# Induced attention and a squared-ReLU feed-forward: elementwise steps over four f-tiles, one transpose per unit, list-scheduled order

## The chip, the cores and the metric

The kernel runs on one core of a Trainium2 chip. The metric is the device time of one execution in microseconds (us), here the median of three runs. The engines of the core are TensorE (PE; PEld is its weight load), VectorE (DVE), ScalarE (ACT), GpSimd (POOL) and SyncE (SP, which issues the DMAs). Each works through its own instructions in the order in which the program issues them, and they wait for each other on semaphores.

## What is computed

From `x` (4 x 12480 x 128), 32 inducing points and the two matrices of a feed-forward layer (128 x 2048 and 2048 x 128):

```python
def mab(q, kv):
    s = scale * (q @ kv.transpose(0, 2, 1))
    s = s - s.max(-1, keepdims=True)
    a = np.exp(s)
    a /= a.sum(-1, keepdims=True) + 1e-09
    return a @ kv
h = mab(I, x)          # first attention: inducing points over all tokens
y = mab(x, h)          # second attention: tokens over the inducing points
...
h = np.maximum(y @ w_in, 0.0)
return (h * h @ w_out)
```

`x` and the inducing points are float32; the weights reach the kernel as float64 words and are turned into float32 on the chip. Nearly all arithmetic is in the two products of the feed-forward layer.

## The kernel before

A batch of 12480 tokens is cut into 13 **units** of 960 tokens, a unit into two **blocks** of 480, the hidden width 2048 into 16 **f-tiles** of 128. There are 52 units. The main loop runs over batches and units; in unit u of batch b the engines also do the first attention of unit u of batch b+1 and the second attention's weights of the next unit. Batch 0's first attention and the conversion of the weights stand ahead of the loop.

- **Feed-forward** (`ffn_block`). The tile `hw` is h @ w_in, split in a rounded part and its rest; `st` holds the second attention's weights, split likewise, with the parts stacked on the 128 partitions as (hi, lo, hi, lo). For each pair of f-tiles two *wide* products (L508, 480 columns) fill a PSUM tile `h`. ACT takes `r` = relu(h) (L515) and `g` = r squared (L522), both 128 x 960; DVE or POOL rounds `g` to `hi` (L593 or L595); DVE forms `lo` = g - hi (L530). Six *narrow* products (L543) add up hi x wo_hi, hi x wo_lo and lo x wo_hi in the PSUM tile `op`. One pair of each unit (marked "f" in `HI`) is not split: its two narrow products take `g` and `wo_f` in plain float32. Of a unit's other 15 pairs POOL rounds 5, DVE 10. At a block's end `op` is copied (`ot`), transposed (`otp`, L569) and scaled into `osb` (L577), which SP stores.
- **Second attention** (`second_unit`): four products `s` (L420, 32 columns of the array each), copied, transposed (`s2t`), the softmax's maximum, difference and exponential (`d`), then POOL writes the rounded weights *twice* and DVE and POOL their rest, so that `sk` holds the stack (hi, lo, hi, lo). Four transposes for each block (`ap`, L477; eight in a unit) turn it, and one copy per block gives `st`.
- **First attention** (`first_unit`): eight transposes `xtp`, four products `sp` (L278), maximum, exponential, two transposes `ep`, eight products `hp` (L324, 32 columns each), and an update of the running sum. `s`, `sp` and `hp` use 32 of the array's columns; everything else uses them all.
- **Order.** Each step is put at a position on a clock of pairs of f-tiles by tables of numbers (`S_MAIN`, `T_MAIN`, `AT_G2` and others); the program sorts the steps by that position and issues them so. Buffers: two PSUM tiles for `h` (a pair each), two for `op`, two banks for all else; in SBUF 3 of `r`, 4 of `g`, 4 of `hi`, 3 of `lo`, each a pair.

Of the kernel before, what the change touches and what calls it, by code (L numbers as in the profile page):

```python
# [24 lines left out]
BLK = UNIT // 2   # tokens of a block, the width of the feed-forward products  # L25


@with_exitstack
def induced_attention_then_squared_relu_ffn(
# [17 lines left out]
    # engines, by pair of f-tiles in the first and the second block of a unit; "f": not split  # L47
    SQ = ('aaaaaaaa', 'aaaaaaaa')   # of the square
    HI = ('vpvpvvpf', 'vvpvvpvv')   # of the rounding
    # engines that empty PSUM  # L50
    XT, XT_EARLY, ET, SS, ST, OT = 'av', 'aa', 'a', 'v', 'av', 'vv'
    RB, GB, HB, LB = 3, 4, 4, 3
    AT_G1, AT_SQA, AT_SQV, AT_HIP, AT_HIA, AT_HIV, AT_LO, AT_G2, AT_G2D = -1.4, 1.05, 0.8, 1.1, 0.7, 1.2, 2.05, 3.3, 0.16
    AT_HI = {"p": AT_HIP, "a": AT_HIA, "v": AT_HIV}
    T_START = (-0.2, 0.3, 0.6, 0.7, 1.5, 1.7, 2.0, 2.4, 3.2, 3.3, 4.1, 4.5)
    T_MAIN = (1.1, 2.2, 2.9, 4.2, 7.2, 7.7, 8.02, 10.3, 10.5, 11.1, 13.4, 13.5)
    E_START = (-0.3, 0.0, 0.6, 0.8, 0.9, 1.0, 1.8, 2.9, 4.4, 4.8, 5.1, 6.1, 6.7, 7.6, 8.0)
    E_MAIN = (0.1, 0.6, 0.7, 1.4, 1.7, 2.1, 2.6, 5.2, 6.8, 8.5, 9.2, 9.3, 10.4, 11.1, 12.9)
    S_MAIN = (0.1, 1.8, 3.0, 3.2, 3.92, 5.2, 5.3, 6.02, 7.1, 7.2, 7.62, 8.1, 9.52, 9.6, 10.1, 10.3, 11.9)
    S_LAST = (0.4, 0.6, 2.7, 3.1, 4.62, 5.2, 5.8, 6.62, 6.9, 7.6, 7.62, 8.1, 8.62, 9.7, 10.0, 14.0, 14.5)  # L60
    S_START = (1.9, 2.1, 2.6, 3.2, 4.36, 4.75, 5.2, 5.26, 5.95, 6.0, 6.31, 6.75, 6.91, 7.35, 7.45, 8.85, 9.95)
    START, T_END, T_FFN, T_NEXT = 1.2, 3.5, 9, 8.5
    W_START = ((1.7, 0.306), (3.3, 0.42), (5.9, 0.504), (8.0, 0.588), (10.6, 0.5), (13.5, 0.35), (15.5, 0.847), (19.8, 0.425))
    O_MAIN = (0.0, 2.2, 2.5)
    AT_S2, AT_S1 = 0.05, 0.05
# [9 lines left out]
    ps_m = ctx.enter_context(tc.tile_pool(name="ps_m", bufs=2, space=PSUM))  # L75

# [3 lines left out]
    # token p * (N / TS) + j of a batch lies on partition p of sub-tile j  # L80
# [14 lines left out]
    # same_m[(q m), (k m')] = (m == m')  # L95
# [8 lines left out]
    # lane_q[(q m), q'] = (q == q')  # L104
# [13 lines left out]
    plan = []  # L118

    def at(t, fn):  # L120
        plan.append((t, len(plan), fn))
# [4 lines left out]
    # w_out's tiles for the products that are not split  # L126
    FULL = [p for p in range(NP) if "f" in (HI[0][p], HI[1][p])]
    wo_f = const.tile([P, 2 * max(len(FULL), 1), C], F32, name="wo_f")
# [6 lines left out]
    def weights(name, load, use, t0, step):  # L135
# [6 lines left out]
        shape = [P, WCH]  # L142

# [36 lines left out]
        def low():  # L180
            v["b"] = tile_of("b", F32)
            nc.vector.scalar_tensor_tensor(
                v["b"], v["w"][:, :, 0].bitcast(U32), 2.0 ** -52, v["power"].bitcast(F32),
                ALU.mult, ALU.mult,
            )
            use(v["a"].bitcast(F32), v["b"])

        at(t0 - 1.5, words)
        for i, fn in enumerate((clamp, size, flush, field, sign, power, low)):
            at(t0 + step * i, fn)  # L190
# [11 lines left out]
    def load_weights():  # L202
        n = F // WCH
        at(-10, open_stage)
        for k in range(n):
            sl = slice(k * WCH, (k + 1) * WCH)

            def load(t, sl=sl):
                nc.sync.dma_start(t, w_in[:, sl].bitcast(I32).rearrange("p (n two) -> p n two", two=2))

            def use(a, b, sl=sl):
                nc.gpsimd.tensor_add(w_in_sb[:, sl], a, b)

            weights(f"i{k}", load, use, *W_START[k])
        for k in range(n):
            m = WCH // C

# [6 lines left out]
            def use(a, b, k=k):  # L224
                hi = wo_hi[:, k * m:(k + 1) * m, :].rearrange("p f c -> p (f c)")
                lo = wo_lo[:, k * m:(k + 1) * m, :].rearrange("p f c -> p (f c)")
                for i, p in enumerate(FULL):
                    if m * k <= 2 * p < m * (k + 1):
                        sl = slice((2 * p - m * k) * C, (2 * p - m * k + 2) * C)
                        nc.gpsimd.tensor_add(  # L230
                            wo_f[:, 2 * i:2 * i + 2, :].rearrange("p f c -> p (f c)"),
                            a[:, sl], b[:, sl],
                        )
                nc.scalar.copy(hi, a)
                nc.gpsimd.tensor_sub(a, a, hi)
# [8 lines left out]
    # lane (q m): inducing point m over the sub-tiles 2q and 2q + 1 of each unit  # L244
    def first_unit(b, u, t0, ahead, times, early=False):
        v = {}
        n = f"{b}_{u}"
        s = state.setdefault(b, {"xt": []})

        def load():  # L250
            v["xn"] = load_x(b, u, pools["early"] if early else xn_pool)

        def turn(k):
            if k == 0:
                v["xt"] = xt_pool.tile([C, UNIT], F32, tag="xt", name=f"xt_{n}")
                s["xt"].append(v["xt"])
            if not early:
                v["tp"] = bank(f"xtp_{n}_{k}")
            else:
                v["tp"] = ps_o.tile([P, 512], F32, tag="o", name=f"xtp_{n}_{k}")  # L260
            tp = v["tp"]
            for t in range(4):
                nc.tensor.transpose(  # L263
                    tp[:, t * TS:(t + 1) * TS], v["xn"][:, 4 * k + t, :], ident[:TS, :TS]
                )

        def turned(k):
            part = v["xt"][:, k * BLK:(k + 1) * BLK]
            copy((XT_EARLY if early else XT)[k], part, v["tp"][:, :BLK])

        def score():
            if early:
                v["sp"] = ps_h.tile([P, 2, 512], F32, tag="h", name=f"sp_{n}")[:, 0, :]
            else:
                v["sp"] = bank(f"sp_{n}")
            sp = v["sp"]
            for q in range(Q):
                nc.tensor.matmul(  # L278
                    sp[q * M:(q + 1) * M, :2 * TS], indT,
                    v["xt"][:, q * 2 * TS:(q + 1) * 2 * TS], start=True, stop=True,  # L280
                )

        def top():
            v["mx"] = tiny.tile([P, 1], F32, tag="mx", name=f"mx_{n}")
            nc.vector.tensor_reduce(v["mx"], v["sp"][:, :2 * TS], axis=AX.X, op=ALU.max)  # L285

        def shift():
            # the maximum so far, times -scale
            v["neg"] = tiny.tile([P, 1], F32, tag="neg", name=f"neg_{n}", bufs=4)
            if u:  # L290
                v["before"] = s["neg"]
                nc.vector.scalar_tensor_tensor(
                    v["neg"], v["mx"], -scale, s["neg"], ALU.mult, ALU.min
                )
            else:
                nc.vector.tensor_scalar_mul(v["neg"], v["mx"], -scale)
            s["neg"] = v["neg"]

        def power():
            v["z"] = tiny.tile([P, 1], F32, tag="z", name=f"z_{n}")  # L300
            v["e"] = att.tile([P, 2 * TS], F32, tag="e1", name=f"e1_{n}")
            nc.scalar.activation(
                v["e"], v["sp"][:, :2 * TS], AF.Exp, bias=v["neg"], scale=scale, accum_out=v["z"]
            )
            if u:
                v["fade"] = tiny.tile([P, 1], F32, tag="fade", name=f"fade_{n}")
# [346 lines left out]
```

## Time and profile before

| | before |
|---|---|
| median of three runs | 1799.92 us (1798.96 to 1800.03) |
| span of the profiled execution | 1796.8 us |
| PE, DVE, ACT, POOL busy | 98%, 90%, 91%, 25% |

The profiled execution's own time isn't given apart from its span, first instruction to last; the median lies 3.1 us above the span. Busy time on PE overstates the work, since successive matmuls overlap; so the rows on PE below are pieces of the chain that ended last, in which every stretch of time is counted once. ACT's and DVE's instructions overlap a little too (one starts some 0.1 us before the end of the one ahead of it).

### The profile page before, as it was taken

What the parts mean: (1) busy time and instruction counts of PE and PEld (TensorE: products, weight loads), DVE (VectorE), ACT (ScalarE), POOL (GpSimd) and SP (SyncE); (2) the same over time, 40 slices, a digit from 0 to 9 for tenths busy, and PEclk for the clock granted to TensorE, in tenths of its full rate; (3) what the DMA queues carried; (4) which work ended last, traced back from release to release, by engine and by line L of the source; (5) the groups of instructions that cost most, each with busy time, mean ns of one, the idle gap of its engine ahead of it and who ended that gap; (6) DMA issues with size and microseconds to landing.
All of it is one profiled execution on the core that took longest, in us unless ns stands there. A gap on an engine that the chain in (4) does not pass through costs nothing.

```text
span 1796.8 us, 27067 instructions
## 1 busy us (share of the span) xinstructions
PE 1766.7 (98%) x9729; PEld 1422.9 (79%) x9729; DVE 1620.0 (90%) x2315; ACT 1628.0 (91%) x2070; POOL 442.8 (25%) x439
## 2 busy tenths in 40 slices
PE   7799999999999999999999999999999999999998
PEld 4478888888778888888878888888887888888887
DVE  6899989999989989989989989989989999999998
ACT  5699999999899999999988999999999999999997
POOL 1312222222222222222221222222222323233231
PEclk9899999999999999999999999999999999999999
DMA  8200100100100110100100110110100000000000
GB/s 214 57 23 23 44 23 23 45 23 23 45 23 23 37 31 23 45 23 23 45 23 23 28 39 23 35 33 23 38 19 12 23 12 23 12 16 19 12 23 23
DMA packets 16912, 57.07 MB, mean 32 GB/s; under 512 B 1704, under 2 KB 3784, under 8 KB 16776
## 3 DMA queue, kind: packets, MB, share of 16 engines
q1 hardware_dynamic: 16776, 55.34, 11.5%
q8 instruction: 76, 1.25, 0.3%
q14 instruction: 60, 0.49, 0.1%
HBM read 29.77 MB, written 25.56 MB: 31 GB/s over the span
## 4 chain that ended last, share of the span: by engine, by line
PE 95%; DVE 2%; DMA 1%; issue 0%; ACT 0%; SPq 0%; POOL 0%; ACTq 0%; DVEq 0%
PE op L543 62%; PE h L508 20%; PE otp L569 3%; PE ap L477 2%; PE xtp L263 2%; PE s L420 2%; PE hp L324 1%; PE sp L278 1%; PE wp L393 1%; DMA words_i<-in_moe_w_in_dram 1%; PE s2t L432 1%; DMA words_o<-in_moe_w_out_dram 1%; PE ep L312 1%; DVE lo L530 0%; DVE mx L285 0%
## 5 line engine op out<-in xcount | busy, mean ns | idle before, releaser
L530 DVE TENSOR_TENSOR lo<-g,hi 128x960 fp32r<-128x960 f32 x780 | 941.9, 1214 | 68.6 <-POOL hi L595 39.1
L515 ACT ACTIVATE r<-h 128x960 f32<-128x960 f32 x832 | 812.0, 976 | 96.8 <-PE h L508 93.7
L522 ACT ACTIVATE g<-r 128x960 f32<-128x960 f32 x832 | 839.6, 1009 | 0.0
L595 POOL TENSOR_SCALAR hi<-g 128x960 fp32r<-128x960 f32 x260 | 282.8, 1088 | 1112.0 <-ACT g L522 1058.1
L543 PE MATMUL op<-hi,wo_hi 128*128 128x480 f32 x1560 | 520.1, 407 | 0.0
L508 PE MATMUL h<-st,hw 128*128 128x480 f32 x1664 | 507.7, 386 | 0.0
L543 PE MATMUL op<-lo,wo_hi 128*128 128x480 f32 x1560 | 479.4, 383 | 0.0
L543 PE MATMUL op<-hi,wo_lo 128*128 128x480 f32 x1560 | 476.2, 381 | 0.0
L593 DVE CAST hi<-g 128x960 fp32r<-128x960 f32 x520 | 374.1, 719 | 3.4 <-ACT g L522 3.4
L543 PEld LDWEIGHTS op<-hi,wo_hi 128*128 128x128 f32 x1560 | 284.4, 189 | 91.7 <-issue 58.7
L508 PEld LDWEIGHTS h<-st,hw 128*128 128x128 f32 x1664 | 306.1, 189 | 47.7 <-issue 3.9
L543 PEld LDWEIGHTS op<-hi,wo_lo 128*128 128x128 f32 x1560 | 293.7, 188 | 43.6
L543 PEld LDWEIGHTS op<-lo,wo_hi 128*128 128x128 f32 x1560 | 293.5, 188 | 41.4 <-DVE lo L530 0.2
L595 POOL TENSOR_SCALAR sk<-d 120x256 fp32r<-120x256 f32 x104 | 102.5, 1001 | 86.3 <-ACT d L446 86.3
L593 DVE COPY ot<-op 128x480 f32<-128x480 f32 x104 | 67.9, 653 | 59.8 <-PE op L543 59.7
L543 PE MATMUL op<-g,wo_f 128*128 128x480 f32 x208 | 100.7, 565 | 0.0
L477 PEld LDWEIGHTS ap<-identr,sk 120*128 120x128 f32 x416 | 62.9, 192 | 26.2 <-issue 20.0
L477 PE MATMUL ap<-identr,sk 120*128 120x120 f32 x416 | 76.3, 306 | 2.0 <-POOL sk L595 2.0
L577 DVE TENSOR_TENSOR osb<-otp,zz 120x512 f32<-120x512 f32 x104 | 70.7, 680 | 2.9 <-PE otp L569 2.2
L263 PE MATMUL xtp<-ident,xn 120*128 120x120 f32 x416 | 63.9, 279 | 8.2 <-DMA xn<-in_x_dram 4.0
L263 PEld LDWEIGHTS xtp<-ident,xn 120*128 120x128 f32 x416 | 51.2, 147 | 22.3 <-ACT xt L591 5.1
L569 PE MATMUL otp<-ident,ot 128*120 128x128 f32 x416 | 63.8, 276 | 0.8 <-DVE ot L593 0.8
(89 smaller groups left out, 867.3 us busy)
## 6 DMA issues: line engine op xcount, KB each, us to landing
xn<-in_x_dram SPq DMA_DIRECT2D x52, 480.0 KB, 5.7
out_dram<-osb SPq DMA_DIRECT2D x52, 480.0 KB, 3.7
words_i<-in_moe_w_in_dram SPq DMA_DIRECT2D x4, 512.0 KB, 6.7
words_o<-in_moe_w_out_dram SPq DMA_DIRECT2D x4, 512.0 KB, 5.0
ind_sb<-in_inducing_dram SPq DMA_DIRECT2D x1, 16.0 KB, 1.7
```

What stands on the lines that cost most here:

```text
L263: nc.tensor.transpose(tp[:, t * TS:(t + 1) * TS], v["xn"][:, 4 * k + t, :], ident[:TS, :TS])
L420: nc.tensor.matmul(sp[q * M:(q + 1) * M, :2 * TS], s["hT"][:, :M], xt[:, q * 2 * TS:(q + 1) * 2 * TS], start=True, stop=True,)
L477: nc.tensor.matmul(ap[:, q * TS:(q + 1) * TS], v["sk"][:, k * Q + q].rearrange("t a k m -> t (a k m)"), identr[:TS, :TS], start=(q == 0), ...
L508: nc.tensor.matmul(v["hp"][:, i, :BLK], s["hw"][:, f * P:(f + 1) * P], s["st", u, k], start=True, stop=True,)
L515: nc.scalar.activation(v["r"], v["hp"][:, :, :BLK], AF.Relu)
L522: nc.scalar.activation(v["g"], v["r"], AF.Square)
L530: nc.vector.tensor_sub(v["lo"], v["g"], v["hi"])
L543: nc.tensor.matmul(w["op"][:, :BLK], wo[:, f, :], v[part][:, i, :], start=(p == 0 and j == 0), stop=(p == NP - 1 and j == len(steps) - 1),)
L569: nc.tensor.transpose(tp[:TS, q * P:(q + 1) * P], w["ot"][:, q * TS:(q + 1) * TS], ident)
L577: nc.vector.tensor_mul(s["osb", u].rearrange("t (q k) c -> t k q c", k=2)[:, k], w["tp"][:TS, :].rearrange("t (q c) -> t q c", q=Q), s["zz ...
L593: nc.vector.tensor_copy(dst, src)
L595: nc.gpsimd.tensor_scalar(dst, src, 1.0, 0.0, ALU.mult, ALU.add)
```

## The change

The parts, as the diff has them:

1. **Four f-tiles.** The relu still takes a pair (128 x 960) but writes into one half of a tile `g` of four f-tiles; the square is taken in place over 128 x 1920; `hi` and `lo` are formed over 128 x 1920, all on DVE. Buffers: 3 of `g`, 2 of `hi`, 2 of `lo`, each four f-tiles; `r` is gone. No pair is left unsplit: `wo_f` and its products are gone, and each unit has 96 narrow products of the split kind (90 before, and 2 in float32).
2. **One transpose.** `sk` is written once, as (block, hi/lo, m), by one rounding on ACT or DVE and one subtraction on DVE; four transposes in a unit instead of eight give both blocks' weights on 64 partitions each; one copy makes `sw`; four DMAs from SBUF to SBUF, issued by SP, write `st` with the stack doubled. POOL has no part in the main loop but the `sums` of each batch's end.
3. **Grouped narrow products.** `s` and `sp` of a unit go into one bank (`na`) and, with the eight `hp` of the first attention's unit before (`nb`), stand in a row on PE.
4. **Order.** A class `Plan` takes the steps with an engine (or a choice of ACT and DVE), a duration, a due time and what they need, and a greedy list scheduler fixes the order and the choice. Copies of `op` go to ACT in 99 of 104 cases (before, all to DVE); of `xt` 66 of 104 (before 65); of `sw` 17 of 52 (of `st` before, 52 of 104); the rounding of `sk` 46 of 52.

```diff
+    def run(self):
...
+                    key = (0.0 if start <= free[e] + 40.0 else start, t.due, t.order)
...
-    RB, GB, HB, LB = 3, 4, 4, 3
+    GB, HB, LB = 3, 2, 2
+    PERIOD, START, T_MAIN, NARROW, STEP = 32000.0, 2600.0, 66000.0, 6000.0, 1700.0
...
         def high():
-            v["sk"] = att.tile([TS, G, 2, 2, M], F32R, tag="sk", name=f"sk_{n}")
-            for k in range(2):
-                copy("p", v["sk"][:, :, k, 0, :], v["d"])
+                v["sk"] = att.tile([TS, Q, 2, 2, M], F32R, tag="sk", name=f"sk_{n}")
+                copy(th, v["sk"][:, :, :, 0, :], v["d"].rearrange("t (k q) m -> t q k m", q=Q))
...
-        def back(k):
-            v["ap"] = ap = bank(f"ap_{n}_{k}")
+            def back():
+                v["ap"] = ap = bank(f"ap_{n}")
                 for q in range(Q):
...
+            def spread():
+                st = att.tile([P, 2, BLK], F32R, tag="st", name=f"st_{n}")
+                for k in range(2):
+                    for j in range(2):
+                        nc.sync.dma_start(
+                            st[j * 64:(j + 1) * 64, k, :].bitcast(F32),
+                            v["sw"][k * 64:(k + 1) * 64, :].bitcast(F32),
+                        )
+                s["st", u] = st
...
+    def narrow(second, f, g, due, step, begun=None):
...
+            if second:
+                second.score(v["a"][:, :2 * TS])
+            if f:
+                f.score(v["a"][:, 2 * TS:4 * TS])
+            if g:
+                v["b"] = bank(f"nb_{g.n}")
+                g.mix(v["b"][:, :C])
...
             def relu():
-                v["r"] = pools["ffn"].tile([P, 2, BLK], F32, tag="r", name=f"r_{n}_{p}", bufs=RB)
-                nc.scalar.activation(v["r"], v["hp"][:, :, :BLK], AF.Relu)
+                    nc.scalar.activation(v["g"][:, 2 * i:2 * i + 2, :], c["hp"][:, :, :BLK], AF.Relu)
...
             def square():
-                    nc.scalar.activation(v["g"], v["r"], AF.Square)
+                nc.scalar.activation(v["g"], v["g"], AF.Square)
...
+            th = add("DVE", 1070, high, due + 5700, [sq], port=True, takes=[bhi], reads=[bg])
+            tl = add("DVE", 2076, low, due + 7800, [th], port=True, takes=[blo], reads=[bg, bhi])
...
+    for t in plan.run():
+        t.fn()
```

On PE in mid batch before, `s` of the next unit between narrow products of the block (names are tile_unit_block..., the batch left out):

```order
L508 MATMUL h_7_0_1_8396<-st_7_0_8269,hw_5477 128x480 x2
L543 MATMUL op_6_1_8303<-hi_6_1_4_8338,wo_lo 128x480 x2
L543 MATMUL op_6_1_8303<-lo_6_1_4_8370,wo_hi 128x480 x2
L420 MATMUL s_1_8_8409<-xt_8_3575,hT_5475 32x240 x4
L543 MATMUL op_6_1_8303<-hi_6_1_5_8375,wo_hi 128x480 x2
L508 MATMUL h_7_0_2_8418<-st_7_0_8269,hw_5477 128x480 x2
L543 MATMUL op_6_1_8303<-hi_6_1_5_8375,wo_lo 128x480 x2
```

And on PE in the changed kernel, where the three narrow groups of a unit stand:

```order
L755 MATMUL h_3_0_0_5915<-st_3_5793,hw_4764 128x480
L795 MATMUL op_2_1_5874<-hi_2_1_1_5892,wo_lo 128x480 x2
L599 MATMUL na_4_5923<-xt_4_1755,hT_4762 32x240 x4
L403 MATMUL na_4_5923<-xt_4_5818,indT 32x240 x4
L457 MATMUL nb_3_5932<-xn_3_5066,et_3_5724 32x128 x8
L795 MATMUL op_2_1_5874<-hi_2_1_1_5892,wo_lo 128x480 x2
L755 MATMUL h_3_0_1_5952<-st_3_5793,hw_4764 128x480
```

The groups that stood in three places of a unit, with full-width products on both sides, now stand in one; and a wide product stands between each two pairs of narrow ones.

On ACT in mid batch before, relu (L515) and square (L522) in turn:

```order
L515 ACTIVATE r_3_0_1_6940<-h_3_0_1_6912 128x960
L522 ACTIVATE g_3_0_0_6944<-r_3_0_0_6918 128x960
L515 ACTIVATE r_3_0_2_6965<-h_3_0_2_6934 128x960
L522 ACTIVATE g_3_0_1_6969<-r_3_0_1_6940 128x960
L591 COPY xt_4_6947<-xtp_4_0_6948 128x480
L515 ACTIVATE r_3_0_3_6988<-h_3_0_3_6957 128x960
L522 ACTIVATE g_3_0_2_6992<-r_3_0_2_6965 128x960
```

And on ACT in the changed kernel at the same stage, relu L763, square L774:

```order
L763 ACTIVATE g_3_0_1_5981<-h_3_0_2_5962 128x960
L763 ACTIVATE g_3_0_1_5981<-h_3_0_3_5974 128x960
L763 ACTIVATE g_3_0_2_5997<-h_3_0_4_5987 128x960
L429 ACTIVATE e_2_4_6011,z_4_6010<-na_4_5923,neg_4_5995 128x240
L432 ACTIVATE fade_4_6013<-neg_3_5685,neg_4_5995 128x1
L774 ACTIVATE g_3_0_1_5981<-g_3_0_1_5981 128x1920
L224 COPY et_4_6034<-ep_4_6023 120x256
L630 ACTIVATE d_4_6038<-d_4_6038 120x256
L224 CAST sk_4_6047<-d_4_6038 120x8x32
L224 COPY ot_2_1_6054<-op_2_1_5874 128x480
```

A square now covers two relus, and the copy `ot` and the rounding `sk` have moved here from DVE and POOL.

On SP in mid batch before, a load of `x` and a store of a unit's result in turn:

```order
L583 DMA out_dram<-osb_4_7622 120x1024
L86 DMA xn_7_7809<-in_x_dram 120x1024
L583 DMA out_dram<-osb_5_7993 120x1024
L86 DMA xn_8_8180<-in_x_dram 120x1024
L583 DMA out_dram<-osb_6_8364 120x1024
```

And on SP in the changed kernel:

```order
L830 DMA out_dram<-osb_2_5903 120x1024
L675 DMA st_4_6103<-sw_4_6087 64x480 x4
L369 DMA xn_7_6260<-in_x_dram 120x1024
L830 DMA out_dram<-osb_3_6213 120x1024
L675 DMA st_5_6413<-sw_5_6397 64x480 x4
L369 DMA xn_8_6570<-in_x_dram 120x1024
```

The four DMAs of a unit's weights stand behind the store of the unit two before, and ahead of a load.

## Rows read from the trace of the kernel before

**Rows 1.** Section 1 of the page: busy us (share of the span) xinstructions, by engine

```profile
PE 1766.7 (98%) x9729; PEld 1422.9 (79%) x9729; DVE 1620.0 (90%) x2315; ACT 1628.0 (91%) x2070; POOL 442.8 (25%) x439
```

**Rows 2.** The chain that ended last, 100 to 1300 us: shares by line

```profile
by line: PE op L543 63.8%; PE h L508 20.4%; PE otp L569 3.0%; PE xtp L263 2.5%; PE ap L477 2.3%; PE hp L324 1.7%; PE s L420 1.6%; PE sp L278 1.5%; PE ep L312 0.7%; PE wp L393 0.6%; PE s2t L432 0.6%; DVE lo L530 0.6%; DVE hw L400 0.1%; DVE o
```

**Rows 3.** DVE timeline, the copy of a finished block: start us, us, instruction [idle before]

```profile
163.12 0.66 DVE L593 COPY ot<-op 128x480 f32<-128x480 f32 x1 [1.30 <-PE op L543]
...
430.32 0.66 DVE L593 COPY ot<-op 128x480 f32<-128x480 f32 x1 [1.32 <-PE op L543]
...
602.52 0.66 DVE L593 COPY ot<-op 128x480 f32<-128x480 f32 x1 [1.32 <-PE op L543]
...
1425.80 0.65 DVE L593 COPY ot<-op 128x480 f32<-128x480 f32 x1
...
1641.96 0.65 DVE L593 COPY ot<-op 128x480 f32<-128x480 f32 x1
```

**Rows 4.** The chain, 426 to 436 us: start us, us on the chain, engine and line

```profile
426.51 0.40 PE ap L477 x4
...
429.48 1.24 PE op L543 x4
...
431.15 1.31 PE op L543 x6
...
433.98 0.57 PE hp L324 x16
```

**Rows 5.** The chain, 0 to 100 us: as in group 4

```profile
19.84 0.54 PE sp L278 x8
20.39 0.54 PE hp L324 x16
...
71.98 0.97 ACT r L515
```

**Rows 6.** PE timeline, 60 to 80 us: columns as in group 3

```profile
68.21 0.99 PE L477 MATMUL ap<-identr,sk 120*128 120x120 f32 x4 [1.98 <-POOL sk L595]
```

**Rows 7.** Groups by line and form: count | busy us, mean ns | idle us before, releasers

```profile
L530 DVE TENSOR_TENSOR lo<-g,hi 128x960 fp32r<-128x960 f32 x780 | 941.9, 1214 | 68.6 <-POOL hi L595 39.1 <-DVE zz L460 0.8 <-PE op L543 0.6
L522 ACT ACTIVATE g<-r 128x960 f32<-128x960 f32 x832 | 839.6, 1009 | 0.0
L515 ACT ACTIVATE r<-h 128x960 f32<-128x960 f32 x832 | 812.0, 976 | 96.8 <-PE h L508 93.7 <-ACT g L522 0.2
...
L593 DVE CAST hi<-g 128x960 fp32r<-128x960 f32 x520 | 374.1, 719 | 3.4 <-ACT g L522 3.4
...
L595 POOL TENSOR_SCALAR hi<-g 128x960 fp32r<-128x960 f32 x260 | 282.8, 1088 | 1112.0 <-ACT g L522 1058.1 <-PE h L508 48.3 <-PE op L543 5.7
...
L593 DVE COPY ot<-op 128x480 f32<-128x480 f32 x104 | 67.9, 653 | 59.8 <-PE op L543 59.7
...
L593 DVE CAST st<-ap 128x480 fp32r<-128x480 f32 x52 | 33.7, 649 | 3.2 <-PE ap L477 3.2
...
L591 ACT CAST st<-ap 128x480 fp32r<-128x480 f32 x52 | 29.3, 563 | 26.1 <-PE ap L477 25.9
...
L469 DVE TENSOR_TENSOR sk<-d,sk 120x256 fp32r<-120x256 f32 x52 | 21.9, 421 | 0.0
...
L446 ACT ACTIVATE d<-d 120x256 f32<-120x256 f32 x52 | 21.3, 410 | 0.0
```

**Rows 8.** DVE timeline, 905 to 908 us: columns as in group 3

```profile
906.08 1.16 DVE L530 TENSOR_TENSOR lo<-g,hi 128x960 fp32r<-128x960 f32 x1
907.15 0.65 DVE L593 CAST hi<-g 128x960 fp32r<-128x960 f32 x1
```

**Rows 9.** Waits, 400 to 1300 us: who waited for whom: us, times, longest

```profile
ACT r L515 <- PE h L508: 58.4, 108, 0.9
```

**Rows 10.** DMA issues: queue, op, count, size, median us to landing

```profile
out_dram<-osb SPq DMA_DIRECT2D x52, 480.0 KB, 3.7
...
ind_sb<-in_inducing_dram SPq DMA_DIRECT2D x1, 16.0 KB, 1.7
```

More of the change, by code (lines that the diff above doesn't have):

```diff
@@ L238, in load_weights @@
-            weights(f"o{k}", load, use, *W_START[n + k])
-        at(t_main - 0.3, open_ffn)
-    state = {}
[L245 to L264, printed above, removed]
-                )
[L267 to L276, printed above, removed]
@@ new lines, in split, with rest @@
+                def split():
+                    nc.scalar.copy(hi, v["a"].bitcast(F32))
+                def rest():
+                    a = v["a"].bitcast(F32)
+                    nc.gpsimd.tensor_sub(a, a, hi)
+                    nc.gpsimd.tensor_add(lo, a, v["b"])
+                t = add("ACT", 530, split, due, needs, **kw)
+                return add("POOL", 2300, rest, due, [t], **kw)
+            outs.append(weights(f"o{k}", load, use, due[n + k]))
+        return ins, outs
+    state = {}
@@ L299, in power @@
[L299 to L306, printed above, removed]
-                nc.scalar.activation(v["fade"], v["before"], AF.Exp, bias=v["neg"], scale=-1.0)
@@ new lines, in first_end @@
+        bl, bj = Buffer("m"), Buffer("m")
+        t = add("DVE", 130, lanes, due, [last.shifted])
+        t = add("PE", 70, gather, due, [t], takes=[bl])
+        t = add("DVE", 80, least, due, [t], reads=[bl])
+        t = add("ACT", 200, share, due, [t])
+        t0 = add("DVE", 200, spread, due, [t])
+        t1 = add("POOL", 700, sums, due, [s["summed"].summed])
+        t = add("PE", 200, join, due + step, [t0, t1], takes=[bj])
+        t = add("DVE", 325, safe, due + step, [t], reads=[bj])
@@ new lines, in first_end @@
+        t = add("DVE", 990, invert, due + step, [t])
+        s["joined"] = add("DVE", 210, joined, due + step, [t], reads=[bj])
+        s["wide"] = []
+        for k in range(F // 512):
+            bw = Buffer("m")
+            d = due + 2 * step + k * step
+            t = add("PE", 870, lambda k=k: wide(k), d, [s["joined"], w_ins[k]], takes=[bw])
+            t = add("ACT", 650, lambda k=k: part(k), d, [t], reads=[bw])
+            s["wide"].append(add("DVE", 725, lambda k=k: rest(k), d, [t], reads=[bw]))
@@ L548, in pair @@
-            t = t0 + p
-            for i in range(2):
-                at(t + AT_G1 + 0.01 * i, lambda i=i: wide(i))
-            at(t, relu)
-            at(t + (AT_SQV if SQ[k][p] == "v" else AT_SQA), square)
-            if not full:
-                at(t + AT_HI[HI[k][p]], high)
-                at(t + AT_LO, low)
-            for j in range(len(steps)):
-                at(t + AT_G2 + AT_G2D * j * (6 // len(steps)), lambda j=j: narrow(j))
-        for p in range(NP):
-            pair(p)
+            sq = add("ACT", 1696, square, due + 4000, relus, reads=[bg])
@@ L562, in done @@
+            return last
+        for j in range(NQ):
+            last = quad(j, last)
         def done():
             w["ot"] = att.tile([P, BLK], F32, tag="ot", name=f"ot_{n}")
-            copy(OT[k], w["ot"], w["op"][:, :BLK])
+            copy(td, w["ot"], w["op"][:, :BLK])
         def turn():
@@ L620, in induced_attention_then_squared_relu_ffn, with store @@
-    for _, _, fn in sorted(plan, key=lambda p: p[:2]):
-        fn()
+        def store():
+            nc.sync.dma_start(out_v[b, :, u * NT:(u + 1) * NT, :], s["osb", u])
+        bt = Buffer("m")
+        end = t0 + PERIOD / 2 + 8000
+        td = add(OT[k], (455, 570), done, end + 1000, [last], reads=[bo])
+        t = add("PE", 420, turn, end + 3000, [td], takes=[bt])
+        t = s["out", u, k] = add("DVE", 600, turned, end + 4000, [t, second.zz], reads=[bt])
+        if k == 1:
+            add("SP", 2000, store, end + 6000, [t, s["out", u, 0]])
@@ new lines, in ffn_block @@
+        return w["begun"]
+    units = [(b, u) for b in range(B) for u in range(NU)]
+    w_ins, w_outs = load_weights(W_DUE)
+    firsts = {}
+    for u in range(NU):
+        firsts[u] = First(0, u, 6000 + START * u, early=True)
+        first_alone(firsts[u], 6000 + START * u)
+    t_end = 6000 + START * NU + 4000
+    first_end(0, t_end, 1500)
+    t_main = T_MAIN
+    seconds = {0: Second(0, 0)}
+    firsts[NU] = First(1, 0, t_main)
+    narrow(seconds[0], None, None, t_end + 4000, 800)
+    after_stage = w_ins + w_outs + [firsts[NU - 1].summed]
```

651 lines of the change are left out of this document (415 added, 236 removed).

## The prediction

> **What bounds the kernel now.** I read the busy shares first: PE 98%, DVE 90%, ACT 91%, POOL 25% [rows 1]. Since PE's busy time counts overlapping products, the chain that ended last says more: over 1200 us of the main loop its eleven entries on PE come to 98.7%, and DVE has under 1% [rows 2]. So PE isn't only busy, it is what everything else waits for. ACT's waits say the same: before a relu it stands idle for a wide product, 58.4 us in 900 [rows 9].
>
> The period comes from the copies of finished blocks [rows 3]: eight units from 163.12 to 430.32 give 33.40 us a unit; a whole batch from 163.12 to 602.52 is 439.4, which is 13 units and 5.2 us at the batch's end, where the four products of h @ w_in and the joining of the lanes are added. In the last batch no first attention is left, and seven units from 1425.80 to 1641.96 give 30.88. Three batches of 439.4 and one of 401.4 make 1719.6 us; the first relu starts at 71.98 [rows 5], and the rest of the 1796.8 us span is the end.
>
> Can PE's own prices explain 33.40? Six narrow products in a row take 1.31, so 0.218 each [rows 4]. 32 wide and 90 narrow ones are 26.6. A float32 product counts as two records: four records with one such product and two split ones take 1.24, so it costs 1.24 - 0.44 = 0.80, two of them 1.6. The other entries of the chain (otp, xtp, ap, hp, s, sp, ep, s2t) are 13.9% of a mean 33.8 us (439.4 over 13), 4.7 [rows 2]. Together 32.9; the half microsecond that is left is the passage between narrow groups and full-width products. PE stands still almost nowhere, and a gain must come off PE's own work.
>
> **The change part by part**, on PE, per unit:
>
> - The unsplit pair: two float32 products go (1.6), six split ones come (1.31). Gain 0.3.
> - The transpose of the weights: four instead of eight. Four take 0.40 [rows 4], and ap's 2.3% of 33.8 us is 0.78 for eight [rows 2]. Gain 0.4.
> - The grouping: hp takes 0.57 [rows 4], s and sp 1.6% and 1.5% of 33.8, 0.54 and 0.51 [rows 2]. Ahead of the loop sp and hp stand one behind the other, and each still takes 0.54 [rows 5]; by that, grouping gives 0. On the other side, if four tiles of 32 columns stream at once, eight records of 240 columns should take as long as one product of 480, 0.22; so up to 0.32 of each group would be entry and exit, and two groups of three could lose it: 0.64. I take 0.2, near the lower end, because the row that shows two groups together is the nearest; both ends go into the range.
>
> So 0.9 us less in the 39 units with a first attention, 35.1 us, and 0.7 in the 13 of the last batch, which have one narrow group and nothing to join: 9.1 us. Sum 44.2 us.
>
> That holds only if ACT and DVE still keep ahead of PE, since both now work in larger pieces.
>
> - ACT. Relus stay (812.0). From 256 to 960 elements an activation goes from 410 to 1009 ns [rows 7], 0.851 ns an element, so 1920 elements take 1.83, and 416 squares 759 in place of 839.6. Copies of op, 99 at 0.563 (the price of the 480-column copy of st), add 55.7; 35 copies of st fewer save 19.7; 46 roundings of sk at about 0.41 add 18.9. ACT goes from 1628 to about 1602.
> - DVE. A lo takes 1.16 where POOL isn't in its way [rows 8], and from 256 elements (0.421) [rows 7] that is 1.05 ns an element: 2.17 for 1920, 902.7 for 416. A hi takes 0.65 for 960 [rows 8]; for 1920 between 1.15 (the fixed part of lo, 0.15, saved once) and 1.30 (nothing saved). I take 1.15, as the instruction is of the same kind, one input and no PSUM: 478. So 1381 in place of 941.9 + 374.1 = 1316. The copies of op that leave give back 99 at 0.653, 64.6, and 17 copies of st 11. DVE goes from 1620 to about 1609. POOL's 260 roundings, 1.09 each, are now DVE's; that is why the larger pieces don't make DVE faster in sum.
>
> Over a span of 1756 these are 91% and 92%, where before they were 91% and 90%. In the loop DVE needs 8 x 3.32 = 26.6 for four f-tiles eight times and 228/52 = 4.4 for the rest (this counts the start's work too), 31.0 of a PE unit of 32.5. Its slack is 1.5 us, 0.19 for each group of four f-tiles. At 1.30 a hi the slack is 0.04. That is thin, and the second rival lives on it.
>
> The new wait: the wide products wait for the four DMAs of st, and these for the copy sw. Behind them on SP stand a load of x for a unit three ahead and a store; behind the wide product on PE stands everything. No row shows a copy within SBUF; the nearest are a 16 KB load, 1.7 to its landing, and the 480 KB store, 3.7 [rows 10]. 120 KB lies between; I take 3, and the issue of four on one queue on top of it. In mid batch 46 narrow and 18 wide products, eight xtp and four otp stand on PE between the transposes ap and the first wide product that needs them, 15.3 us by the prices above, so the DMAs are hidden with 9 us to spare. The store ahead of them on SP takes 3.7 and fits in that. At a batch's end only 8.1 us stand there: hidden at 3, not with a late store in front. I take 0 for the three batch ends and up to 3 us each in the range. Before the first unit only eight xtp, 0.84, stand there. But there PE waits 1.98 for POOL's rounding of sk today [rows 6], and that goes. Between -1 (landing at 1.7) and +5 (landing at 3.7 and four issues in a row), I take +2.
>
> The end: the last group passes through a square, a hi and a lo that are longer by 0.8, 0.5 and 1.0. Partly PE's remaining products cover it: between 0 and 2.3, I take 1.
>
> 1799.9 - 44.2 + 2 + 1 = 1758.7. The sum is made against the profiled span of 1796.8 us; the median is 3.1 us above it, and I leave that distance as it is. **Forecast: 1759 us**, and by the ends of the unknown costs 1742 to 1776.
>
> **The rivals.**
>
> 1. *The narrow groups give more.* If entry and exit are what they cost, the gain is 0.64 in place of 0.2, 17 us more in 39 units: 1742. For it speaks that a group of eight records takes 2.5 times as long as its columns need; against it, that the prologue's pair shows nothing of it. The Trainium skill, page "TensorEngine Tiling (Array Packing)", section "Key Properties", has it that a change of the tiling mode drains TensorE; by that rule four of six such changes in a unit go, and this rival would be the forecast. The trace bears it out half: the half microsecond that no entry explains is there, the two groups in a row at full price too. Chance 0.08.
>
> 2. *Coarser hand-offs, slower than before.* A hi can't start before a whole square of 1920 is done, a lo not before the whole hi, a narrow product not before its 1920 columns; there are 2 buffers of hi and lo, of four f-tiles. Place: DVE, between the square and the hi, eight times a unit. Price: whatever DVE waits beyond 0.19 us per group comes off PE, 0.1 us per group being 8 x 52 x 0.1 = 42 us. The gain of 0.9 a unit is eaten at 0.19 + 0.11 = 0.30 us; from there the kernel is slower. At 0.4 it takes 1759 + 0.21 x 416 = 1846. For it: three engines within 9% of full, in an order fixed beforehand. Against it: DVE waited 3.4 us in all for ACT ahead of its 520 roundings [rows 7], at a similar load, and the other small steps of DVE stand between the pieces and fill such waits. Chance 0.12.
>
> 3. *Half of it.* The same waits at about 0.25 us per group, or a hi at 1.30 and some waits: 0.06 x 416 = 25 us back, 1784. Chance 0.16.
>
> 4. *It does not do what it says*: a product that waits for its own bank, so that the groups cost what they cost apart, and DMAs that come late at every unit. Lateness in mid batch would have to pass 9 us first. About no change, 1800. Chance 0.04.
>
> **How the numbers follow.** The forecast gets the rest, 0.60. The range from 1742 to 1792 holds it, the first rival's time and the third's; what is left out is the second, the fourth and a share of the third. A measurement of this kernel tells 0.2% from no change, some 3.6 us. Faster: forecast, first and third rival, 0.84; within 0.2%: the fourth, 0.04; slower: 0.12.
>
> **What would show it.** In the profile after, the chain should still be PE at over 95%, with no entry of a float32 product, ap at half its share, and the period of a unit at 32.5 (30.2 in the last batch). Three narrow groups in a row at 1.45 or less say that the 0.2 is right; at 1.65 grouping gave nothing, at 1.1 rival 1 is right. The square should take 1.83, lo 2.17, hi 1.15. If DVE or ACT stand in the chain with several per cent, or PE waits for hi or lo by name, it is rival 2 or 3. A wait of a wide product for st in mid batch would refute the 9 us to spare; at batch ends and in the first unit a few microseconds wouldn't surprise. The prediction is most wrong if a hi of 1920 elements takes well over 1.30, since DVE then sets the pace.

## The result: 1777.4 us, half of the forecast gain

| | before | after |
|---|---|---|
| median of four runs | 1799.97 us (1798.96 to 1800.16) | 1777.42 us (1776.82 to 1777.97) |
| ratio to before | | 0.9879, 95% interval 0.9865 to 0.9893 |
| span of the profiled execution | 1796.8 us | 1775.8 us |

The change gains 22.5 us. The forecast was 1759, 41 us less than before. The time lies inside the range from 1742 to 1792, but above the 1776 that the unknown costs alone gave; the stretch above that was there for the third rival.

Section 1 of the page after (busy us, share of the span, count), which answers to [rows 1]:

```profile
PE 1736.6 (98%) x9625; PEld 1415.7 (80%) x9625; DVE 1641.0 (92%) x1736; ACT 1652.7 (93%) x1765; POOL 22.2 (1%) x22
```

The chain that ended last, from 100 to 1300 us, which answers to [rows 2]:

```profile
by line: PE op L795 43.5%; PE h L755 14.3%; ACT g L763 14.3%; issue 9.4%; ACT g L774 7.0%; PE otp L815 2.0%; PE xtp L388 1.5%; PE ap L660 1.2%; PE na L599 1.0%; PE nb L457 0.8%; PE na L403 0.7%; ACT xt L224 0.7%; PE s2t L616 0.7%; PE ep L43
```

PE's busy share is the same 98%, and says nothing. The chain says it: where before nearly all of it was PE, ACT's relu (L763), its square (L774) and the pieces of "issue" between them now hold 30.7%. PE no longer runs at its own pace.

The stores of finished units on SP give the period (start us, us, instruction), as the copies in [rows 3] did:

```profile
579.51 0.35 SPq L830 DMA_DIRECT2D out_dram<-osb  x1
612.37 0.35 SPq L830 DMA_DIRECT2D out_dram<-osb  x1
...
875.19 0.35 SPq L830 DMA_DIRECT2D out_dram<-osb  x1
...
1009.59 0.35 SPq L830 DMA_DIRECT2D out_dram<-osb  x1
...
1434.13 0.34 SPq L830 DMA_DIRECT2D out_dram<-osb  x1
...
1652.81 0.34 SPq L830 DMA_DIRECT2D out_dram<-osb  x1
```

Eight units from 612.37 to 875.19 are 32.85 us each (33.40 before, 32.5 forecast). A batch from 579.51 to 1009.59 is 430.1 (439.4 before). Seven units of the last batch from 1434.13 to 1652.81 are 31.24 each: 0.36 *longer* than before (30.88), where 30.2 was forecast. Three times 9.3 gained and 13 times 0.36 lost make 23 us gained, near the 21.0 between the spans.

The pieces themselves came out as forecast (count | busy us, mean ns | idle before, releaser; and the DMAs with KB each and median us to landing):

```profile
L774 ACT ACTIVATE g<-g 128x1920 f32<-128x1920 f32 x416 | 759.4, 1826 | 5.1
L778 DVE CAST hi<-g 128x1920 fp32r<-128x1920 f32 x416 | 480.1, 1154 | 78.8 <-ACT g L774 75.3
...
st<-sw SPq DMA_DIRECT2D x208, 120.0 KB, 2.6
```

Square 1.83 (1.83 forecast), hi 1.15 (1.15), DMA 2.6 (3); lo took 2.15 (2.17). So none of these operations was misjudged. What was misjudged is who waits for whom. Waits from 400 to 1300 us (who for whom: us, times, longest), to be set beside [rows 9]:

```profile
DVE hi L778 <- ACT g L774: 37.0, 49, 1.3
PEld h L755 <- ACT g L763: 25.8, 74, 0.7
...
PE h L755 <- ACT g L763: 6.0, 22, 0.3
```

PE's wide product (here its weight load, PEld) waits for a relu 74 times; in the kernel before, no wide product waits for a relu in that stretch. There are two PSUM tiles `h`; a wide product needs one that a relu has emptied. One such place, the chain from 829 to 834 us (start us, us on the chain, engine and line):

```profile
829.83 0.99 ACT g L763
...
830.86 1.69 issue
832.56 0.96 ACT g L763
...
833.56 0.48 PE h L755
```

and ACT's timeline there (start us, us, instruction):

```profile
829.83 0.98 ACT L763 ACTIVATE g<-h 128x960 f32<-128x960 f32 x1
830.84 1.81 ACT L774 ACTIVATE g<-g 128x1920 f32<-128x1920 f32 x1
832.56 1.81 ACT L763 ACTIVATE g<-h 128x960 f32<-128x960 f32 x2
```

A relu ends at 830.8. The next one stands behind a square of 1.81 and can't start before 832.56; its PSUM tile is free at 833.52, and the wide product that needs it starts at 833.56. The 1.69 of "issue" is the square. PE has other products to do for most of that time; what it loses is the last part, 0.30 us in its own timeline:

```profile
833.56 0.48 PE L755 MATMUL h<-st,hw 128*128 128x480 f32 x1 [0.30 <-ACT g L763]
```

Before, a square held ACT 1.01 us [rows 7] and every relu had one in front of it; now two relus follow each other and then comes a gap of about 1.7 to 1.8, with the same two tiles to bridge it.

### The profile page after: what moved, and what is told of

The parts are those of the page before. It is cut to its first block, busy times and chain, and to the rows that moved or that the text cites. A ratio compares the mean times of both kernels' runs of the same rounds, so it can differ in the third digit from the quotient of the medians.

```text
span 1775.8 us, 24582 instructions
## 1 busy us (share of the span) xinstructions
PE 1736.6 (98%) x9625; PEld 1415.7 (80%) x9625; DVE 1641.0 (92%) x1736; ACT 1652.7 (93%) x1765; POOL 22.2 (1%) x22
## 4 chain that ended last, share of the span: by engine, by line
PE 67%; ACT 20%; issue 9%; DVE 2%; DMA 1%; SPq 0%; ACTq 0%; DVEq 0%
PE op L795 43%; PE h L755 15%; ACT g L763 13%; ACT g L774 6%; PE otp L815 2%; PE xtp L388 1%; PE ap L660 1%; PE na L599 1%; DMA xn<-in_x_dram 1%; PE wp L559 1%; PE s2t L616 1%; PE na L403 1%; DVE lo L782 1%; PE ep L437 1%; ACT xt L224 1%
## 5 line engine op out<-in xcount | busy, mean ns | idle before, releaser
L782 DVE TENSOR_TENSOR lo<-g,hi 128x1920 fp32r<-128x1920 f32 x416 | 895.6, 2153 | 13.0 <-DVE hi L778 0.9
L763 ACT ACTIVATE g<-h 128x960 f32<-128x960 f32 x832 | 783.0, 982 | 47.8 <-PE h L755 42.1
L774 ACT ACTIVATE g<-g 128x1920 f32<-128x1920 f32 x416 | 759.4, 1826 | 5.1
L755 PE MATMUL h<-st,hw 128*128 128x480 f32 x1664 | 644.3, 388 | 15.4 <-ACT g L763 12.5
L778 DVE CAST hi<-g 128x1920 fp32r<-128x1920 f32 x416 | 480.1, 1154 | 78.8 <-ACT g L774 75.3
L795 PE MATMUL op<-hi,wo_hi 128*128 128x480 f32 x1664 | 481.8, 382 | 0.2 <-DVE hi L778 0.2
L224 ACT COPY ot<-op 128x480 f32<-128x480 f32 x99 | 55.8, 564 | 27.1 <-PE op L795 26.9
L815 PEld LDWEIGHTS otp<-ident,ot 128*120 128x120 f32 x416 | 48.9, 137 | 15.6 <-ACT ot L224 6.6
L224 ACT COPY xt<-xtp 128x480 f32<-128x480 f32 x66 | 36.3, 555 | 13.7 <-PE xtp L388 13.6
L660 PE MATMUL ap<-identr,sk 120*128 120x120 f32 x208 | 29.5, 265 | 0.0
```

The source lines that it names most:

```text
L224: ENG[task.by](dst, src)
L660: nc.tensor.matmul(ap[:, q * TS:(q + 1) * TS], v["sk"][:, q].rearrange("t k a m -> t (k a m)"), identr[:TS, :TS], start=(q == 0), stop=(q ...
L755: nc.tensor.matmul(c["hp"][:, l, :BLK], s["hw"][:, f * P:(f + 1) * P], s["st", u][:, k, :], start=True, stop=True,)
L763: nc.scalar.activation(v["g"][:, 2 * i:2 * i + 2, :], c["hp"][:, :, :BLK], AF.Relu)
L774: nc.scalar.activation(v["g"], v["g"], AF.Square)
L778: nc.vector.tensor_copy(v["hi"], v["g"])
```

## The experiments

Four theories were set against each other. **A**: PE waits for relus that stand behind the long squares. **B**: PE's own work came out dearer than forecast. **C**: DVE, with its pieces of 1.15 and 2.15 us, sets the pace (the place of rival 2). **D**: the planner frees a buffer 60 ns after its last use in its own reckoning, too early for the chip, and so orders some steps badly.

**Short squares.** The order stays; ACT's load falls from 93% to 62%.

```diff
-                nc.scalar.activation(v["g"], v["g"], AF.Square)
+                nc.scalar.activation(v["g"][:, :, :8], v["g"][:, :, :8], AF.Square)
```

> The changed kernel with every square over 32 of its 1920 elements, all instructions in the same order on every engine (the square of the rest is left out). It takes some 600 us of work off ACT and nothing off PE. Theory A, wide products on PE wait for a relu that stands on ACT behind a 1.7 us square: these waits (31.8 us in 900 us of the middle batches, 20.4 in 350 us of the last) go, and the time falls to 1715 to 1735 us. Theory B, PE's own work is what the period consists of and the forecast's prices of it were too low: 1770 us or more. Theory C, DVE sets the pace: 1770 us or more too, with PE waiting for hi or lo.

Measured: 1746.94. Its stores:

```profile
571.58 0.35 SPq L830 DMA_DIRECT2D out_dram<-osb  x1
603.90 0.35 SPq L830 DMA_DIRECT2D out_dram<-osb  x1
...
862.72 0.35 SPq L830 DMA_DIRECT2D out_dram<-osb  x1
...
996.17 0.35 SPq L830 DMA_DIRECT2D out_dram<-osb  x1
...
1444.02 0.34 SPq L830 DMA_DIRECT2D out_dram<-osb  x1
...
1656.22 0.34 SPq L830 DMA_DIRECT2D out_dram<-osb  x1
```

32.35 us a unit in mid batch, 30.31 in the last batch, 424.6 a batch. In the chain from 100 to 1300 us PE's lines again make nearly all:

```profile
by line: PE op L795 65.0%; PE h L755 21.3%; PE otp L815 2.7%; PE xtp L388 2.5%; PE na L599 1.6%; PE nb L457 1.3%; PE ap L660 1.2%; PE na L403 1.2%; PE s2t L616 0.7%; PE ep L437 0.7%; PE wp L559 0.6%; DVE lo L782 0.4%; DVE hi L778 0.3%; issu
```

So the squares cost 5.5 us in each of three batches and 0.93 in each of the last 13 units, 28.6 us of the 30.6 between the spans. B and C, at 1770 or more, are out. A's own range, 1715 to 1735, was missed by 12 us: it took every recorded wait for lost time, while at the place above the weight load waits 0.71 us (its row at 833.56 in PEld's timeline) and PE loses 0.30. PE's pace here is better than forecast in mid batch (32.5) and about as forecast in the last (30.2). The run doesn't tell whether the length of a square or ACT's load as a whole is the trouble; the halves below are for that.

**The kernel before with short squares**, to see whether it, too, lost time to ACT.

```diff
...
-                v["g"] = pools["ffn"].tile([P, 2, BLK], F32, tag="g", name=f"g_{n}_{p}", bufs=GB)
+                v["g"] = v["r"]
...
-                    nc.scalar.activation(v["g"], v["r"], AF.Square)
+                    nc.scalar.activation(v["g"][:, :, :8], v["g"][:, :, :8], AF.Square)
```

> The kernel before with squares of 16 columns in place of 960 (in place in the relu's tile, of which there are 7): most of the squaring is left out, the order of all work stays. It tells PE's own pace before, as the run with short squares did for the changed kernel (1746.9, 32.34 us a unit in mid batch, 30.25 in the last). Theory A (before, PE waited for nobody; the wait for ACT came with the long square): 1790 to 1800, period 33.3 to 33.4. Rival: the kernel before lost time to relus behind squares as well, some 10 to 25 us of it: 1770 to 1787, period 33.1 or less; then the change of PE's own work is smaller than it looks.

Measured: 1796.87, and ot copies 33.40 us apart, as in [rows 3]:

```profile
343.58 0.65 DVE L593 COPY ot<-op 128x480 f32<-128x480 f32 x1
...
443.78 0.65 DVE L593 COPY ot<-op 128x480 f32<-128x480 f32 x1
```

Three units in 100.20 us. Before, the squares cost 1 us or nothing; with the chain of [rows 2], the prediction's start, that PE alone bounds that kernel, holds. With the squares out of the way in both kernels the span falls by 49.9 us (1795.1 to 1745.2), where the forecast, with 3 us for the start and the end, had 41.2.

**DVE lighter.** `lo` as a copy of g, the subtraction left out; the order stays.

```diff
-                nc.vector.tensor_sub(v["lo"], v["g"], v["hi"])
+                nc.vector.tensor_copy(v["lo"], v["g"])
```

> The changed kernel with lo taken as a copy of g (one input) in place of g minus hi, all instructions in the same order; the subtraction is left out. DVE's lo should fall from 2.15 to about 1.15 us, 416 us of work in all. Theory C, DVE sets the pace: below 1750 us. Theories A and B: within 8 us of 1777, since PE waits for hi or lo only 1.7 us in 900.

Measured: 1775.95, 1.5 us less, with a lo of 1.15 us. From 400 to 1300 us the weight loads of wide products still wait 24.7 us for relus, against 25.8. C falls: DVE isn't what is waited for.

**A later release in the plan.** 150 ns in place of 60 in the planner's reckoning.

> The changed kernel with one number of the planner changed: a buffer counts as free 150 ns after its last reader's end in place of 60; so a wide product is put later among the narrow ones. The trace has it free 0.15 us later than the planner assumes (a relu planned at 855 ns ends 0.98 us after its start). Theory D, the order puts wide products a little too early and PE, which takes them in order, waits each time: 1755 to 1768 us. Theory A without D, B and C: within 5 us of 1777.

Measured: 1769.28 (0.9842 of before, 0.9826 to 0.9858). A unit takes 32.80 in mid batch and 30.83 in the last: 13 x 0.41, some 5 of the 8 us gained, are in the last batch. D is a part of it, 8 us at this one value; on top of the halves below it is 9.

**Squares in halves, planned apart**: each of 960 columns, behind its own relu, the rest by the planner.

```diff
-            sq = add("ACT", 1696, square, due + 4000, relus, reads=[bg])
-            th = add("DVE", 1070, high, due + 5700, [sq], port=True, takes=[bhi], reads=[bg])
+            sq = [add("ACT", 890, lambda i=i: square(i), due + 3100 + 900 * i, [relus[i]], reads=[bg]) for i in range(2)]
+            th = add("DVE", 1070, high, due + 5700, sq, port=True, takes=[bhi], reads=[bg])
```

> The changed kernel with the square taken as two instructions of 960 elements, each after its own relu, in the planner's new order; 416 more instructions on ACT, about 35 us more work there. Theory A in the form that the length of one square blocks the relus: 1750 to 1765 us. Theory A in the form that ACT is simply too full: 1785 us or more. Theories B and C: within 5 us of 1777.

Measured: 1757.21 (0.9769 of before, 0.9754 to 0.9784). Section 1 of its page:

```profile
PE 1724.5 (98%) x9625; PEld 1422.7 (81%) x9625; DVE 1673.6 (95%) x1824; ACT 1651.9 (94%) x2093; POOL 24.0 (1%) x22
```

and its waits from 400 to 1300 us:

```profile
PEld h L755 <- ACT g L763: 4.9, 16, 0.6
```

1651.9 us of ACT against 1652.7, and 20 us faster; so ACT's load over the whole run isn't what costs the time. The load is equal because the planner moved 88 smaller steps, on balance, from ACT to DVE, most of them copies of op; DVE went from 1641.0 to 1673.6. A unit takes 32.13 in mid batch (32.85 in the changed kernel), and 30.93 in the last (31.24). There only a third of the 0.93 comes back, and ACT is busy 207.15 of the 210 us from 1430 to 1640; so for the last batch it isn't excluded that ACT is too full.

The order differs too, since the planner ran again, and so the next run.

**Squares in halves, in place**: the same two instructions, one behind the other where the one stood.

```diff
-                nc.scalar.activation(v["g"], v["g"], AF.Square)
+                for i in range(2):
+                    h = v["g"][:, 2 * i:2 * i + 2, :]
+                    nc.scalar.activation(h, h, AF.Square)
```

> The changed kernel with each square issued as two instructions of 960 columns, one right behind the other at the place where the one of 1920 stood; the order of all work is that of the changed kernel, and no relu stands between the halves. The run with halves that were planned apart, each behind its own relu, took 1757.2; this one tells whether the shorter instruction helped there or the relu that can pass between. Theory (a relu has to wait until both halves are done, so PSUM comes free no earlier): no gain, and the fixed part of 416 more instructions, 416 x (2 x 1.01 - 1.83) = 79 us of ACT, makes it 1778 or more, up to 1830 if all of it lands on PE. Rival (a long instruction is itself the trouble, wherever its neighbours stand): 1765 or less.

Measured, in one run: 1784.81, slower than the changed kernel. ACT's timeline:

```profile
831.42 1.03 ACT L763 ACTIVATE g<-h 128x960 f32<-128x960 f32 x1
832.28 1.96 ACT L776 ACTIVATE g<-g 128x960 f32<-128x960 f32 x2
834.07 1.89 ACT L763 ACTIVATE g<-h 128x960 f32<-128x960 f32 x2
```

A relu still waits for both halves. From the start of the first to the next relu it is 1.79 us (832.28 to 834.07), with one long square 1.72 (830.84 to 832.56). Instructions in a row overlap, so the price of two halves was 0.07 us a group here, and in all ACT's busy time rose by 16.4 us (1669.1), 0.04 a group, not the 0.19 that I had put against it. The shorter instruction by itself gains nothing. Planned apart, a relu can pass between the halves, and the weight loads' waits for relus fell from 25.8 to 4.9 us; that passage is the likely cause of the gain, though no run separates it from the rest of the new order.

**Both: halves and the later release.**

> The changed kernel with the square in two halves of 960 columns, each behind its own relu (1757.2 alone), and 150 in place of 60 ns between a buffer's last use and its next in the planner (1769.3 alone, 8 us less than the changed kernel, mostly in the last batch). If both shorten the same waits, of which few are left: 1753 to 1759. If the planner's later release still helps in the last batch, where a unit takes 30.0 and 31.8 in turn: 1745 to 1752. PE's own pace with this work is 1747 by the run with short squares.

Measured: 1748.22 (1747.54 to 1748.66), 0.9721 of before (0.9706 to 0.9735), the fastest whole kernel. Its chain from 100 to 1300 us:

```profile
by line: PE op L795 64.9%; PE h L755 21.3%; PE otp L815 2.7%; PE xtp L388 2.5%; PE na L599 1.6%; PE nb L457 1.4%; PE ap L660 1.2%; PE na L403 1.2%; PE ep L437 0.7%; PE s2t L616 0.6%; PE wp L559 0.5%; ACT g L763 0.5%; ACT g L774 0.4%; PE hp 
```

and its waits of wide products for relus, 400 to 1300 us:

```profile
PEld h L755 <- ACT g L763: 0.3, 2, 0.2
```

25.8 us of waits have become 0.3 there, and the time is near that of the run with short squares. In part that is chance: a unit takes 32.12 in mid batch, 0.23 *below* that run, so its 32.35 was no floor for PE, and 30.75 in the last, 0.44 above it. There (1430 to 1640 us) DVE is busy 98% and ACT 97%; that rest I left open.

**The narrow groups apart**, on top of the short squares, so that ACT is out of the way.

```diff
-            narrow(seconds[w + 1], f, g, t_u + NARROW, STEP, begun)
+            narrow(seconds[w + 1], None, None, t_u + NARROW, STEP, begun)
+            if g:
+                narrow(None, None, g, t_u + NARROW + 7000, STEP)
+            if f:
+                narrow(None, f, None, t_u + NARROW + 14000, STEP)
```

> The changed kernel with short squares (most of the squaring left out, as in the run of 1746.9), and the narrow groups s, hp and sp of a unit apart again, in three places with full-width products on both sides. So ACT is out of the way and the difference to 1746.9 (32.34 us a unit in mid batch) is what grouping saves. By the forecast 0.2 us in 39 units: 1755, period 32.5. If a group's entry and exit are what it costs (rival 1) 0.64: 1772, period 33.0. If grouping saves nothing: 1745 to 1749, period 32.3 to 32.4.

Measured: 1763.64, 16.7 us more than with them together; a unit takes 32.79 on the mean, 0.44 more. That lies between the forecast's price (1755) and rival 1's (1772). The planner ran again here, so the order of the other work differs too. The chain with the groups apart (nb is the tile that hp fills):

```profile
609.64 0.59 PE nb L457 x16
610.23 0.64 PE op L795 x2
...
614.82 0.54 PE na L403 x8
...
631.47 0.54 PE na L599 x8
632.01 0.64 PE op L795 x2
```

and together, in the run with short squares:

```profile
620.87 0.54 PE na L599 x8
621.41 0.41 PE na L403 x8
621.81 0.47 PE nb L457 x16
622.28 0.64 PE op L795 x2
```

The second and third group of a row lose 0.13 and 0.12, and two pairs of products, which take 0.64 behind a group, lose 0.2 each, as pairs elsewhere take 0.44 [rows 4]. These entries come to 0.65; the period shows 0.44. Where the other 0.2 goes isn't settled. The three in a row take 1.42.

**The unsplit pair alone**, on the kernel before.

```diff
-    HI = ('vpvpvvpf', 'vvpvvpvv')
+    HI = ('vpvpvpvp', 'vvpvvpvv')
```

> The kernel before with one thing changed: the pair of each unit that was not split is split like the others (its rounding on POOL, its rest on DVE), so 52 x 2 float32 products become 52 x 6 split ones. It prices that term of the forecast alone. By the forecast's prices (two of 0.80 us against six of 0.218) 0.3 us of PE's work go in each of 52 units: 1784, between 1780 and 1788, the period of a unit in mid batch 33.1 in place of 33.40. If two float32 products cost no more than 1.31 together, no change: 1797 to 1801. Rival: DVE gets 52 more subtractions of 1.21, 63 us, and goes to about 1683, 94%; if that makes it late for PE, 1795 or more with DVE in the chain.

Measured: 1822.04, slower (1.0134 of before, 1.0118 to 1.0151). Yet the stores in mid batch are closer together:

```profile
587.29 0.34 SPq L583 DMA_DIRECT2D out_dram<-osb  x1
...
852.47 0.34 SPq L583 DMA_DIRECT2D out_dram<-osb  x1
```

33.15 a unit, 0.25 less than before, near the forecast (0.3). The loss is all in the last batch, where copies of ot at 1436.06 and 1602.76, five units apart, give 33.34 in place of 30.88; that is the rival named above. The chain from 1430 to 1640 is hardly PE any more:

```profile
by line: issue 22.8%; DVE lo L530 18.8%; POOL hi L595 14.6%; DVE hi L593 13.0%; POOL sk L595 8.0%; ACT g L522 6.9%; ACT r L515 5.6%; PE op L543 3.8%; DVE ot L593 1.9%; DVE st L593 1.9%; PE s L420 1.6%; PE h L508 1.3%; DVE zz L460 0.3%; DVE 
```

Busy us from 1430 to 1640 of PE, PEld, DVE, ACT, POOL, in the kernel before and in this run:

```profile
1430.00:1640.00 210.00, 210.00 (x1035) 174.25 (x1034) 193.16 (x259) 200.18 (x231) 61.55 (x53) 1.00 0.06 17
1430.00:1640.00 210.00, 202.70 (x969) 157.92 (x969) 201.92 (x245) 186.96 (x216) 73.06 (x57) 1.00 0.06 15
```

and the group of DVE's hi in that stretch, in the same order (count | busy us, mean ns | idle before):

```profile
L593 DVE CAST hi<-g 128x960 fp32r<-128x960 f32 x68 | 46.2, 680 | 0.0
L593 DVE CAST hi<-g 128x960 fp32r<-128x960 f32 x63 | 63.1, 1002 | 0.0
```

A hi took 1.00 on DVE there, 0.68 in the kernel before. So the pair in float32 cost PE only 0.25 us a unit, and kept DVE and POOL from holding PE up in the last batch; the term of the forecast was measured in the middle batches alone, and needs a kernel that has that room.

## Why the prediction was half right

**The bound** was read rightly: PE, by its chain, and freeing ACT of its squares changes that kernel by 1 us.

**PE's terms** held, but for grouping. In mid batch 0.25 for the pair (0.3 forecast), 0.4 for ap (its share of the chain is 1.2% of 32.85, 0.39, where it was 0.78), 0.44 for grouping (0.2): 1.08 by parts, 1.05 by the periods (33.40 to 32.35), 0.9 forecast. In the last batch 0.57 (0.7 forecast). A batch's end costs 4.0 with short squares (3.0 in the changed kernel) instead of 5.2, which I had not reckoned with.

**Grouping** is the term that was mis-sized, and the reason is in the row I chose. I took the low end since in [rows 5] sp and hp stand one behind the other at 0.54 each. But sp is the first of the two and has its way in to pay in any case, so only hp could show a saving, and under hp the granted clock fell. Windows of before (busy us of PE, PEld, DVE, ACT, POOL, then the granted clock, DMA share, GB/s):

```profile
15.00:20.00 5.00, 2.10 (x35) 1.44 (x30) 2.85 (x6) 2.54 (x7) 1.30 (x1) 1.00 0.96 260
20.39:20.93 0.54, 0.54 (x17) 0.24 (x10) 0.54 (x4) 0.25 (x1) 0.00 (x0) 0.68 1.01 235
```

PE had stood idle for 2.9 of the 5 us from 15 to 20. In the 0.54 of hp the clock was a mean of 0.68, so it fell within it from 2.4 to 1.2 GHz (0.50 of full speed from 21 to 22 us). This hp can't be set beside 0.57 at full clock; behind another group at full clock it takes 0.47. The upper end, 0.64 from the columns of a group, was nearer to the entries (0.65) though not to the period (0.44). I also had the way out in my hands and did not price it: half a microsecond of a unit that no entry explained, where three exits at 0.2 make 0.6. And the sign that I had set, three groups in a row at 1.45 or less, came true at 1.42 and says nothing of the exits. The Trainium skill, page "TensorEngine Tiling (Array Packing)", section "Key Properties", says that a change of the tiling mode drains TensorE; the runs agree in sign, with a price of 0.13 on the way in and 0.2 on the way out. Rival 1's mechanism is there, with 0.44 of its 0.64; its 1742 also needed the kernel to run at PE's pace.

**"That holds only if ACT and DVE still keep ahead of PE"** is the step that failed. I worked it out from busy shares: ACT 1602 (it became 1652.7), DVE 1609 (1641.0), both below 94%. The sums were 50 and 32 short since I added up durations, while successive instructions overlap by some 0.1 us: with 416 fewer squares, ACT loses 416 overlaps, some 42 us. But that isn't what cost the time in mid batch, as the halves with the same busy time show. A share says that the work fits, not that each piece comes in time. I then looked for the danger at DVE, between square and hi. There DVE does wait, 75.3 us for 416 groups, 0.18 each, just under the 0.19 of slack that I had given it; and from 400 to 1300 us no wait of PE for hi or lo is on the list. What I did not follow is the other hand-off from ACT: the relu gives a PSUM tile *back* to PE. With two tiles, each 0.44 of wide products, and a square of 1.8 that no relu can pass, PE's cover runs out. Rival 3 had nearly the size (1784 for half of it) with the wrong place. So the time came into the range by two errors against each other: PE's own time fell by about 9 us more than forecast, and the waits for ACT, priced at nothing, took 30 back.

**The last batch** shows it most. PE needs 30.3 a unit there and ACT did not follow; of the loop's stretches it is the only one that became slower. I had carried the gain of 0.7 over without asking that batch whether its ACT had room: in [rows 1] a mean of 91% stood over it, while ACT was busy for 200.18 of 210 us there (the first of the two rows of 1430 to 1640 above), 95%. Whether the order or the load holds ACT back there stays open: halves and the later release together came to 30.75.

**The start** was 1.4 us later by its first relu (73.38 against 71.98; 2 forecast), and the wait is the one forecast:

```profile
71.68 1.94 PE L755 MATMUL h<-st,hw 128*128 128x480 f32 x4 [1.43 <-DMA st<-sw]
```

In mid batch no wide product waited for the DMAs, as forecast; the last of the four landed some 10 us ahead of the product that needs it, and 3 to 5 at a batch's end. At the end the chain holds a hi of 1.17 and a lo of 2.17 that PE no longer covers; I did not price them apart.

## What to carry to other kernels

Before an instruction is made longer to save its fixed part, list every buffer that the same engine must give back while it runs, not only what waits for its result; if fewer buffers stand behind it than the consumer uses up in that time, the gain goes into the wait. A list scheduler can hide this, as its plan fits on paper: make the long piece divisible and let the returning step pass between, even if it costs more busy time. And take a price only from a row whose granted clock is that of the place where the price is used.

## What I had not expected of the hardware

Two squares of 960 columns in a row took 1.96 us, one of 1920 took 1.81 to 1.83, and with 416 squares cut in two ACT's busy time rose by 16.4 us. By the means of [rows 7] and of the long square, twice 1.009 less 1.826, it should have been 0.19 a group, 80 us. So most of an activation's fixed part hides behind the instruction ahead of it, and there is little to be saved by making it longer.

A hi of 960 columns took 0.68 us on DVE in the last batch of the kernel before and 1.00 with every pair split, while POOL's own rose from 1.20 to 1.49 us. The share that POOL takes isn't the reason: in the middle batches of the same run, with the same 6 pairs of 16 on POOL, a hi on DVE took 0.67. The long ones are those that meet an instruction of POOL. Of the 63 hi in the last batch's stretch 25 had none beside them and took 0.65; the 38 others took 1.23 on the mean, where the 61 that met one in the middle batches (400 to 1300 us) took 0.74. One of the long ones on DVE, and POOL's beside it:

```profile
1500.11 1.46 DVE L593 CAST hi<-g 128x960 fp32r<-128x960 f32 x1
...
1499.23 1.82 POOL L595 TENSOR_SCALAR hi<-g 128x960 fp32r<-128x960 f32 x1 [2.06 <-ACT g L522]
```

The Trainium skill, page "SBUF — State Buffer", section "SBUF: two separate sides", has DVE and GpSimd share a pair of ports that one holds for a whole instruction; the numbers fit that, but no run here shows the ports themselves.
